# A fused retention and expert kernel: row scales written between two halves of the sums, expert loads moved up, and twenty products of the unit matrix ahead of the first expert

## The chip, the cores and the metric

The kernel runs on one core of one Trainium2 chip. The metric is the device time of one execution in microseconds (us). A core has five engines with an instruction queue of their own: TensorE (PE, with its weight loads as PEld), VectorE (DVE), ScalarE (ACT), GpSimd (POOL) and SyncE (SP), which issues most DMA transfers here. The 16 DMA engines are shared by all queues.

## The reference, cut to what matters

```python
# 1. retention: a decayed running state of k v^T, read with q     -> y [4, 8, 768, 64]
# 2. x = y as 3072 rows of 512; a first layer of 8 experts, each row goes to one:
logits = x @ w_gate;  e_idx = argmax(logits)
gate_w = softmax(logits)[e_idx];  eom = 1 / (1 + exp(-(x @ w_output_gate)))
for e in range(8):
    mask = e_idx == e
    out[mask] = gate_w[mask] * eom[mask, e] * (relu(x[mask] @ w1[e]) @ w2[e])
# 3. a second layer: slots from softmax(out @ phi) over the tokens, 8 experts over
#    the slots, and softmax(out @ phi) over the slots to put them together
```

All of it is float32. Layer 2 is never written out: the kernel folds `w2[e] @ phi` into one matrix per expert (`wp`), so that the logits of layer 3 come straight from the hidden units.

## The kernel before, in words

The order of all work is written out by hand: each engine runs its instructions in the order in which the Python code issues them, and waits on semaphores where data is missing.

**Stage A, up to about 115 us.** 24 tiles of 128 tokens go through the retention. For each group of three tiles the rows (`xr`) and 16 copies of the row's scale (`sv`, 64 bytes a row) are written to a DRAM table `xs` (`x_put`, `scale_put`). While the last tiles run, the first quarter of `w2[e] @ phi` is computed for all eight experts (`first_mm`, `first_copy`) into `fsum`, and written to a DRAM buffer `wps` in two halves of 512 KB.

**The handover, about 112 to 127 us.** `rank` and the products `lp` give each expert its list of tokens (`xidx`). GpSimd then gathers the rows of the first expert from `xs`, 128 rows at a time (`gather`, three tiles `xg`). After that stands a branch around a path for overfull experts, which is not taken (`tc.If(most > 0)`, L868): every engine reads a number and jumps over some hundreds of instructions. Behind the branch SP waits until the three gathers have landed (`after(..., gets[0])`, L1104) before it loads the other three quarters of the first expert's `w2` (`wq_load`, three loads `wt` of 512 KB). PE's first work behind the branch is `x_mm(0)`: twelve transposes `xps` of the scaled rows, four for each gathered tile. ACT and DVE split them into two parts (`x_split`, `xh` and `xl`).

**Stage B, the eight experts, about 127 to 370 us.** An expert has eight units of 128 hidden columns (unit g = 8e + f). A unit needs a weight load `r` (256 KB, `load_w(g + 3)`, three buffers), its split `wh`, `wl` on ACT and DVE (`split_w(g + 2)`, issued at the head of unit g), twelve matmuls `hps` on PE (`l1`, four quarters times three products, PSUM from a pool `ps_h` of two buffers), and a relu on ACT, which frees the PSUM buffer. ACT runs at the head of unit g: the split of unit g + 2, in units 4 and 5 two scalings of the next expert's rows (`x_scale`), and then the relu of unit g. For expert 0, `wq_mm(0)` multiplies the three loads `wt` behind unit 2 and frees their three buffers (`wup`). The loads of expert 1 into the same buffers are issued behind units 3 and 4, and `wq_mm(1)` stands behind unit 6. `part_load(1)` (`wpp`, 128 KB) reads the first quarter back from `wps`.

**Stage C, about 370 us to the end.** The second layer's experts on 32 slots, and the output.

Of the kernel before, what the change touches and what calls it, by code (L numbers as in the profile page):

```python
# [9 lines left out]
F32 = mybir.dt.float32  # L10
# [17 lines left out]
KD = DM // 128  # L28
# [10 lines left out]
IO, UMM, QA = 6, 2, 1  # L39
# [98 lines left out]
def retention_moe_kernel(ctx, tc, qt, kt, kn, vn, gates, moe_w1, moe_w2,  # L138
                         moe2_phi, moe2_w1, moe2_w2, consts, out, dbg=None):
    nc = tc.nc  # L140
# [11 lines left out]
    def con(name, shape=None):  # L152
        o, n = off[name]
        a = cs0[:, o:o + n] if o < ni else cs_a[0][:, o - ni:o - ni + n] if o < na else cs[:, o - na:o - na + n]
        if shape:
            a = a.rearrange("p (a b) -> p a b", b=shape)
        return a

    ident = con("ident")
# [36 lines left out]
    def load_er(k):  # L196
        if k < E:
            er.append(nc.values_load(ordi[0:1, k:k + 1], engines=[mybir.EngineType.SP], min_val=0, max_val=E - 1))
# [3 lines left out]
    def after(inst, earlier):  # L202
        for other in earlier:
            tc.add_manual_dep(inst.ins, other.ins.name,
                              mybir.DependencyInfo(mybir.DependencyClass.Sync, mybir.DependencyReason.DATA),
                              reason="order of transfers")
# [25 lines left out]
    def wq_load(k, q, n, pool, tag):  # L232
        t = pool.tile([128, n * FF], F32, tag=tag, name="wt")
        get = nc.sync.dma_start(out=t, in_=moe_w2[1, bass.ds(er[k], 1), :, q * FF:(q + n) * FF].rearrange("o p d -> (o p) d"))
        for h in range(n):
            wtt[k, q + h] = [t[:, h * FF + g * 256:h * FF + g * 256 + 256] for g in range(4)]
        return get
# [8 lines left out]
    def wq_add(k):  # L246
        nc.vector.tensor_tensor(out=parts[k], in0=wacc.pop(k), in1=parts[k], op=ALU.add)
# [69 lines left out]
    with ExitStack() as pa:  # L317
# [96 lines left out]
        def first_copy(e):  # L414
            nc.scalar.copy(out=fsum[:, e, :], in_=facc.pop(e))
# [133 lines left out]
        def bc(a, n, m=E):  # L549
            return a.unsqueeze(2).to_broadcast([128, n, m])  # L550
# [35 lines left out]
        def gate_scale(i):  # L586
            if i not in ENDS:
                return
            t, n = ENDS[i]
            sm = gs.pop(t)  # L590
            one_ = lambda k: sm[:, k, 0, 0:n]
            nc.vector.tensor_reduce(out=one_(8), in_=sm[:, 6, 0:n, :], axis=AX.X, op=ALU.add)
            nc.vector.tensor_scalar(out=one_(9), in0=one_(7), scalar1=1.0, scalar2=None, op0=ALU.add)
            nc.vector.scalar_tensor_tensor(out=one_(10), in0=one_(8), scalar=1e-9, in1=one_(9), op0=ALU.add, op1=ALU.mult)
            scl[t] = sc2.tile([128, 3, DX - DM], F32, tag="sv", name="sv")
            nc.vector.reciprocal(out=scl[t][:, 0:n, :], in_=bc(one_(10), n, DX - DM))
# [39 lines left out]
        def scale_put(i):  # L636

            if i not in ENDS:
                return
            t, n = ENDS[i]  # L640
            nc.sync.dma_start(out=xs[t * 128:(t + n) * 128, DM:DX].rearrange("(u p) o -> p u o", p=128), in_=scl.pop(t)[:, 0:n, :])
# [52 lines left out]
        i = NTILE - 1  # L694
# [5 lines left out]
        t, n = ENDS[i]  # L700
        past = [base[:, 0, 0:E], run[:, t, :]] + [oh[:, t + u, :] for u in range(n)]
        for o, w, terms in ((key, eights, past), (key, ones, [base[:, 1, 0:E]]), (counts, ones, past)):
            for m, b in enumerate(terms):
                nc.tensor.matmul(out=o, lhsT=w, rhs=b, start=(m == 0 and terms is past),
                                 stop=(m == len(terms) - 1 and (o is counts or terms is not past)), skip_group_check=True)
# [17 lines left out]
            first_mm(e)  # L723
        for e in range(4, E):
            first_copy(e)
        nc.sync.dma_start(out=wps[:, 4:E], in_=fsum[:, 4:E])
        gate_scale(i)
        scale_put(i)
        load_er(0)
        load_w(0)  # L730
        load_w(1)
# [16 lines left out]
        xg, gets = {}, {}  # L748
# [23 lines left out]
    with ExitStack() as pv:  # L772
# [95 lines left out]
        with tc.If(most > 0):  # L868
# [5 lines left out]
            for i in range(NTILE):  # L874
                places.append(nc.gpsimd.indirect_dma_start(
                    out=inv[:, :], out_offset=bass.IndirectOffsetOnAxis(ap=pos[:, i:i + 1], axis=0),
# [12 lines left out]
    wup = ctx.enter_context(tc.tile_pool(name="wup", bufs=KD - QA))  # L889
    with ExitStack() as pb:  # L890
        sp = pb.enter_context(tc.tile_pool(name="sp", bufs=1))
        ps_h = pb.enter_context(tc.tile_pool(name="ps_h", bufs=2, space=PSUM))
# [5 lines left out]
        def x_scale(e, j, vector=False):  # L898
            r = XT[e][j]
            x, s = xg[e][j][0:r, 0:DM], xg[e][j][0:r, DM:DM + 1]  # L900
            if vector:
                nc.vector.tensor_scalar(out=x, in0=x, scalar1=s, scalar2=None, op0=ALU.mult)
            else:
                nc.scalar.activation(out=x, in_=x, func=ACTF.Copy, scale=s)

        def x_mm(e, tags, blocks):

            ps = [ps_1.tile([128, C[e]], F32, tag=tag, name="xps") for tag in tags]
            for j, kk in blocks:
                r = XT[e][j]  # L910
                nc.tensor.transpose(out=ps[kk][:, j * 128:j * 128 + r],  # L911
                                    in_=xg[e][j][0:r, kk * 128:(kk + 1) * 128],
                                    identity=ident[0:r, 0:r])
            return ps
# [156 lines left out]
        def slot_acc(e):  # L1071
            nc.vector.scalar_tensor_tensor(out=acc, in0=acc, scalar=sms.pop(e)[:, 4:5], in1=slo.pop(e), op0=ALU.mult, op1=ALU.add)
# [28 lines left out]

        load_er(1)

        after(wq_load(0, QA, 1, wup, "wu"), gets[0])  # L1104
        for q in range(QA + 1, KD):
            wq_load(0, q, 1, wup, "wu")
        part_load(0)
        for j in range(len(XT[0])):
            if j == 1:
                split_w(0)  # L1110
            x_scale(0, j, j % 2 == 0)
        xps = x_mm(0, "ABCD", [(j, kk) for j in range(len(XT[0])) for kk in range(KD)])
        for ps in xps:
            x_split(0, ps)
        split_w(1)
        for g in range(G):
            e, f = divmod(g, KF)
            if f == 0:
                load_er(e + 2)
            if e + 1 < E and f < len(XT[e + 1]):  # L1120

                gather(e + 1, (f,))
                if f:
                    after(gets[e + 1][f], [relu[-1]])
            split_w(g + 2)
            if e and f == 1:

                if e > 1:
                    slot_acc(e - 2)
                logit_parts(e - 1)  # L1130
            if g < G - 3:
                load_w(g + 3)
            else:
                load_m2(wraw, "r1")
            if g > 3 and g % 2 and len(m2_t) < NPRE:
                load_m2(m2p, "m2", 2)
            if f in (4, 5) and e + 1 < E:
                for j in range(2 * f - 8, min(2 * f - 6, len(XT[e + 1]))):
                    x_scale(e + 1, j)
            if f == KF - 1 and e + 1 < E:  # L1140

                xps = x_mm(e + 1, "ABDr", sorted(((j, kk) for kk in range(KD) for j in range(len(XT[e + 1]))),
                                                 key=lambda b: XT[e + 1][b[0]] < 128))
                l1(g, lambda: [x_split(e + 1, ps) for ps in xps])
            else:
                l1(g)
            behind(e - 1, f)


            if g == UMM:  # L1150
                wq_mm(0, ps_1, "C")
                wq_add(0)
            if f == (1 if e else UMM):
                wq_turn(e, sp.tile([128, KF, NS], F32, tag="wp", name="wp"))
            if e + 1 < E:
                if f == (2 if e else 3):
                    part_load(e + 1)
                if e == 0 and f in (3, 4):
                    for q in ((1, 2), (3,))[f - 3]:
                        wq_load(1, q, 1, wup, "wu")  # L1160
                if f == (3 if e else 6):

                    wq_mm(e + 1, ps_1, "A" if e else "C")
                    wq_add(e + 1)
            if g == KF - 1:
                wq_load(2, 1, 1, wup, "wu")
                wq_load(2, 2, 1, wup, "wu")
            if g == KF:
                wq_load(2, 3, 1, wup, "wu")
            if e and e + 2 < E and 4 <= f < 7:  # L1170
                wq_load(e + 2, f - 3, 1, wup, "wu")
            elif G - 13 < g < G - 9:
                load_m2(wup, "wu", 2)
            if g == G - 6:
                load_w2(e, range(4), xp, "xy")
            if g >= G - 2:

                for i, tag in enumerate(("wh1", "wl1")):
                    load_w2(e, (2 * f - 8 + i,), whl, tag)
            if f == 4:  # L1180
                logits(e, 0)
            if f == 5:

                mask(e)
            if f >= 5:
                h_tr(e, 2 * f - 10)
                h_tr(e, 2 * f - 9)
        e = E - 1
# [30 lines left out]
        for kk in range(KD):  # L1219
            nc.tensor.matmul(out=ps4[:, kk, :], lhsT=acc[:, kk * 128:(kk + 1) * 128], rhs=sw,  # L1220
                             start=True, stop=True, skip_group_check=True)
# [171 lines left out]
```

## Time and profile before

| | |
|---|---|
| Time, median of 3 runs (lowest, highest) | 427.85 us (426.66, 427.98) |
| Time of the profiled execution | 427.91 us |
| Its span in the trace | 426.1 us, so 1.8 us lie around it |
| PE busy | 379.5 us (89% of the span) |
| DVE, ACT, POOL busy | 260.9, 165.6, 108.0 us |
| DMA | 132.96 MB, mean 312 GB/s |
| Granted TensorE clock, mean | 0.963 of full speed |
| Share of the chain that ended last | PE 73%, DVE 9%, DMA 7%, ACT 4% |

PE is the busiest engine and holds most of the chain that ended last. Two stretches stand out in its busy time by slices: one near 115 to 122 us, where it does nothing, and the tail beyond 355 us. The granted clock is at half (1.2 of 2.4 GHz) in the slices after the first of these. Times below are us from the start of the span.

### The profile page before, as it was taken

What the parts mean: (1) busy time and instruction counts of PE and PEld (TensorE: products, weight loads), DVE (VectorE), ACT (ScalarE), POOL (GpSimd) and SP (SyncE); (2) the same over time, 40 slices, a digit from 0 to 9 for tenths busy, and PEclk for the clock granted to TensorE, in tenths of its full rate; (3) what the DMA queues carried; (4) which work ended last, traced back from release to release, by engine and by line L of the source; (5) the groups of instructions that cost most, each with busy time, mean ns of one, the idle gap of its engine ahead of it and who ended that gap; (6) DMA issues with size and microseconds to landing.
All of it is one profiled execution on the core that took longest, in us unless ns stands there. A gap on an engine that the chain in (4) does not pass through costs nothing.

```text
span 426.1 us, 11539 instructions
## 1 busy us (share of the span) xinstructions
PE 379.5 (89%) x4407; PEld 284.7 (67%) x4407; DVE 260.9 (61%) x681; ACT 165.6 (39%) x368; POOL 108.0 (25%) x116
## 2 busy tenths in 40 slices
PE   2989999998639999999999999999999996799990
PEld 2877777786428777777877877787679872225560
DVE  1698989988723276575675664864757655414250
ACT  1532322223324365454545545543555421112232
POOL 2203333321033113043252431620612122020020
PEclk9999999999958999999999999999999999699996
DMA  7999999999958798977969969969778789999998
GB/s 270 403 420 334 307 314 338 304 280 327 251 161 316 222 368 287 385 279 237 403 225 329 376 203 357 358 192 386 248 223 338 238 263 318 388 398 407 392 346 289
DMA packets 68002, 132.96 MB, mean 312 GB/s; under 512 B 10628, under 2 KB 30082, under 8 KB 65634
## 3 DMA queue, kind: packets, MB, share of 16 engines
q1 hardware_dynamic: 61154, 120.17, 80.2%
q0 software_dynamic: 3344, 8.34, 6.5%
q10 hardware_dynamic: 3440, 3.63, 2.6%
q8 instruction: 36, 0.59, 0.6%
q14 instruction: 28, 0.23, 0.2%
HBM read 117.89 MB, written 14.25 MB: 310 GB/s over the span
## 4 chain that ended last, share of the span: by engine, by line
PE 73%; DVE 9%; DMA 7%; ACT 4%; issue 3%; SPq 1%; ACTq 1%; another core or an unknown queue 0%; POOL 0%; POOLq 0%; DVEq 0%
PE hps L933 30%; PE s L447 5%; PE o L480 5%; PE gps L1046 5%; PE fh L1246 4%; PE slo L1068 4%; PE so L1283 3%; PE lps L963 3%; PE wps L243 3%; PE o L471 2%; DMA r<-in_moe_w_dram 2%; DMA raw<-in_qt_dram 2%; PE xps L911 2%; PE st L494 2%; PE g L545 2%
## 5 line engine op out<-in xcount | busy, mean ns | idle before, releaser
L933 PE MATMUL hps<-xh,wh 128*128 128x416 f32 (+2 forms) x256 | 92.9, 363 | 0.1
L933 PE MATMUL hps<-xl,wh 128*128 128x416 f32 (+2 forms) x256 | 90.1, 352 | 0.3 <-DVE xl L921 0.2
L933 PE MATMUL hps<-xh,wl 128*128 128x416 f32 (+2 forms) x256 | 89.5, 350 | 0.0
L223 DVE TENSOR_TENSOR wl<-r,wh 128x512 fp32r<-128x512 f32 x64 | 43.4, 680 | 57.9 <-ACT wh L222 47.3
L938 ACT ACTIVATE h<-hps 128x416 f32<-128x416 f32 (+2 forms) x64 | 32.6, 510 | 68.7 <-PE hps L933 67.1
L222 ACT ACTIVATE wh<-r 128x512 fp32r<-128x512 f32 x64 | 40.2, 630 | 48.9 <-DMA r<-in_moe_w_dram 38.2
L933 PEld LDWEIGHTS hps<-xh,wh 128*128 128x128 f32 x256 | 48.7, 190 | 15.5 <-issue 13.4
L1029 POOL DMA_INDIRECT ctok<-ce,xidx x29 | 30.1, 1040 | 100.9 <-DVE ce L1026 94.5
L933 PEld LDWEIGHTS hps<-xl,wh 128*128 128x128 f32 x256 | 48.8, 190 | 2.2 <-DVE xl L921 1.2
L933 PEld LDWEIGHTS hps<-xh,wl 128*128 128x128 f32 x256 | 48.7, 190 | 0.6
L755 POOL DMA_INDIRECT xg<-xs,xidx x29 | 30.4, 1047 | 70.3 <-ACT h L938 49.5
L457 DVE TENSOR_TENSOR sS<-s,csa 128x512 f32<-128x512 f32 x48 | 30.4, 674 | 14.4 <-PE s L447 14.4
L447 PE MATMUL s<-raw 64*128 64x128 f32 x384 | 31.9, 301 | 8.0 <-DMA raw<-in_qt_dram 7.7
L945 DVE STREAM_TRANSPOSE hB<-h 128x416 f32<-128x416 f32 (+2 forms) x64 | 34.4, 576 | 0.0
L447 PEld LDWEIGHTS s<-raw 64*128 64x128 f32 x384 | 26.7, 201 | 10.7 <-DMA raw<-in_qt_dram 5.5
L480 PE MATMUL o<-sS,raw 128*64 128x128 f32 x384 | 27.1, 285 | 0.0
L512 ACT COPY xT<-o 128x512 f32<-128x512 f32 x24 | 13.9, 580 | 32.0 <-PE o L480 32.0
L429 POOL TENSOR_TENSOR k<-raw,cs 128x512 f32<-128x512 f32 x20 | 21.9, 1110 | 16.4 <-DMA raw<-in_qt_dram 11.1
L911 PE MATMUL xps<-cs,xg 128*128 128x128 f32 (+2 forms) x116 | 15.7, 285 | 9.2 <-ACT wh L222 7.9
L480 PEld LDWEIGHTS o<-sS,raw 128*64 128x64 f32 x384 | 21.2, 140 | 3.7 <-issue 3.4
L1046 PE MATMUL gps<-hB,pd 32*32 32x256 f32 x816 | 19.8, 394 | 3.6 <-DVE pd L1000 3.6
L911 PEld LDWEIGHTS xps<-cs,xg 128*128 128x128 f32 (+2 forms) x116 | 12.8, 148 | 13.6 <-issue 11.7
(178 smaller groups left out, 532.6 us busy)
## 6 DMA issues: line engine op xcount, KB each, us to landing
m<-in_moe_w_dram SPq DMA_DIRECT2D x41, 512.0 KB
wt<-in_moe_w_dram SPq DMA_DIRECT2D x32, 512.0 KB
r<-in_moe_w_dram SPq DMA_DIRECT2D x64, 256.0 KB
w<-in_moe_w_dram SPq DMA_DIRECT2D x64, 256.0 KB
m<-in_moe_w_dram SPq DMA_DIRECT2D x36, 256.0 KB
xs<-xr SPq DMA_DIRECT2D x32, 192.0 KB
raw<-in_kt_dram SPq DMA_DIRECT2D x5, 1024.0 KB
raw<-in_kn_dram SPq DMA_DIRECT2D x5, 1024.0 KB
```

The lines of the kernel that those rows point to most:

```text
L222: nc.scalar.activation(out=hi, in_=t, func=ACTF.Copy)
L223: nc.vector.tensor_tensor(out=lo, in0=t, in1=hi, op=ALU.subtract)
L447: nc.tensor.matmul(out=ps[h][:, p, :], lhsT=kq(i, p, 0)[r], rhs=kq(i, p, 1)[r], start=True, stop=True, tile_position=(64 * h, 0), skip_gro ...
L457: nc.vector.tensor_tensor(out=sS[i][:, h], in0=sps.pop((i, h)), in1=con("dm", 128)[:, 4 * h:4 * h + 4, :], op=ALU.mult)
L480: nc.tensor.matmul(out=o_at(i, p, h), lhsT=vals(i, 2 * p + h), rhs=s[:, h, p, :], start=(i % NCH == 0 and n < 4), stop=True, skip_group_ch ...
L755: gets.setdefault(e, []).append(nc.gpsimd.indirect_dma_start(out=t[0:r, :], out_offset=None, in_=xs[:, :], in_offset=bass.IndirectOffsetOn ...
L911: nc.tensor.transpose(out=ps[kk][:, j * 128:j * 128 + r], in_=xg[e][j][0:r, kk * 128:(kk + 1) * 128], identity=ident[0:r, 0:r])
L933: nc.tensor.matmul(out=ps, lhsT=a[:, kk * 128:(kk + 1) * 128], rhs=x[e][kk][:, 0:c], start=(n == 0), stop=(n == 11))
L938: relu.append(nc.scalar.activation(out=hs[g][:, 0:c], in_=ps, func=ACTF.Relu))
L945: nc.vector.transpose(out=hB[e][:, 0:NB[e], f, :], in_=hs[e * KF + f][:, 0:c].rearrange("p (b t) -> p b t", t=32))
L1029: put = nc.gpsimd.indirect_dma_start(out=ctok[:, :], out_offset=bass.IndirectOffsetOnAxis(ap=xidx[0:r, e, j:j + 1], axis=0), in_=cn[0:r, j ...
L1046: nc.tensor.matmul(out=ps[a][32 * j:32 * j + 32, :], lhsT=pd[q, b, :], rhs=hB[e][q, b].rearrange("p f t -> p (f t)"), start=(i == 0), stop ...
```

## The change

Four things are moved or added.

1. `gate_scale` and `scale_put` of the last group come ahead of the second half of `fsum` in SP's order.
2. The first load of expert 0's three `wt` waits for two gathers of the three.
3. Twenty float32 products of the 128x128 unit matrix with itself are put on PE between the branch and `x_mm(0)`. Nobody reads them. Their tile `idle` takes one of the two buffers of `ps_h`.
4. Expert 1's three loads `wt` are all issued right behind `wq_mm(0)`, in unit 2, not in units 3 and 4.

```diff
             first_copy(e)
+        gate_scale(i)
+
+        scale_put(i)
         nc.sync.dma_start(out=wps[:, 4:E], in_=fsum[:, 4:E])
-        gate_scale(i)
-        scale_put(i)
         load_er(0)
...
-        after(wq_load(0, QA, 1, wup, "wu"), gets[0])
+        after(wq_load(0, QA, 1, wup, "wu"), gets[0][:2])
...
             x_scale(0, j, j % 2 == 0)
+
+        idle = ps_h.tile([128, 512], F32, tag="h", name="idle")
+        for n in range(20):
+            nc.tensor.matmul(out=idle[:, n % 4 * 128:n % 4 * 128 + 128], lhsT=ident, rhs=ident, start=True, stop=True, skip_group_check=True)
         xps = x_mm(0, "ABCD", [(j, kk) for j in range(len(XT[0])) for kk in range(KD)])
...
             if g == UMM:
                 wq_mm(0, ps_1, "C")
                 wq_add(0)
+                for q in range(QA, KD):
+                    wq_load(1, q, 1, wup, "wu")
...
-                if e == 0 and f in (3, 4):
-                    for q in ((1, 2), (3,))[f - 3]:
-                        wq_load(1, q, 1, wup, "wu")
```

On PE, right behind the branch (L868, after the change L869), with `cs` the constants that hold the unit matrix, the changed kernel has:

```order
+L788 COMPARE_AND_BRANCH
+L788 UNCONDITIONAL_BRANCH
+L869 UNCONDITIONAL_BRANCH
+L1116 MATMUL idle<-cs_65 128x128 x20
+L912 MATMUL xps<-cs_65,xg 128x128 x12
+L934 MATMUL hps<-xh,wh_3555 128x384
```

The twenty products stand behind the branch and ahead of the twelve transposes; nothing else moves on PE here.

On SP, at the end of stage A, with `xs<-sv` the scales and `wps<-fsum` the two halves of the sums:

```order
 L649 DMA xs<-xr 32x12x128 x4
 L721 DMA wps<-fsum 128x1024
-L726 DMA wps<-fsum 128x1024
 L641 DMA xs<-sv 128x3x16
+L729 DMA wps<-fsum 128x1024
 L198 TENSOR_LOAD ordi
```

The scales go past one transfer of 512 KB. On DVE no row moves.

On SP, in units 2 to 5 of expert 0 (`r` the weight loads, `wt` the loads for `wq_mm(1)`, `wpp` the first quarter), before, with the load of unit 6 as `r_3706` and that of unit 7 as `r_3733`:

```order
L214 DMA r_3665<-in_moe_w_dram 128x512 [waits DMAHW3_49,DVE_49]
L214 DMA r_3706<-in_moe_w_dram 128x512 [waits DMAHW4_49,DMAHW1_49,DVE_49]
L949 DMA wpp<-wps 128x256 [waits DMAHW5_49,DVE_49]
L234 DMA wt<-in_moe_w_dram 128x1024 [waits DMAHW6_49,PE_49]
L234 DMA wt<-in_moe_w_dram 128x1024 [waits DMAHW7_49,PE_49]
L214 DMA r_3733<-in_moe_w_dram 128x512 [waits DMAHW2_49,DMAHW0_49,Activation_49]
L234 DMA wt<-in_moe_w_dram 128x1024 [waits PE_49]
L214 DMA r_3763<-in_moe_w_dram 128x512 [waits DMAHW3_49,DVE_49]
```

and after the change, with the load of unit 6 as `r_3733` and that of unit 7 as `r_3756`:

```order
L214 DMA r_3686<-in_moe_w_dram 128x512 [waits DMAHW3_49,DVE_49]
L234 DMA wt<-in_moe_w_dram 128x1024 [waits DMAHW5_49,DMAHW4_49,PE_49]
L234 DMA wt<-in_moe_w_dram 128x1024 [waits DMAHW6_49,PE_49]
L234 DMA wt<-in_moe_w_dram 128x1024 [waits DMAHW7_49,PE_49]
L214 DMA r_3733<-in_moe_w_dram 128x512 [waits DMAHW1_49,DVE_49]
L950 DMA wpp<-wps 128x256 [waits DMAHW0_49,DVE_49]
L214 DMA r_3756<-in_moe_w_dram 128x512 [waits DMAHW2_49,Activation_49]
L214 DMA r_3784<-in_moe_w_dram 128x512 [waits DMAHW3_49,DVE_49]
```

The load of unit 6 was ahead of all three `wt` and is now behind them; the load of unit 7 was ahead of one and is now behind all three.

## Rows read from the trace of the kernel before

**Rows 1.** Time by windows: busy us of five engines, clock, DMA share, GB/s.
```profile
115.00:120.00 5.00, 0.00 (x0) 0.00 (x0) 2.04 (x10) 0.00 (x0) 2.02 (x2) 0.83 0.69 197
131.00:132.00 1.00, 1.00 (x5) 1.00 (x5) 0.00 (x0) 0.12 (x1) 0.00 (x0) 0.50 1.01 385
132.00:133.00 1.00, 1.00 (x7) 1.00 (x6) 0.00 (x0) 0.37 (x1) 0.36 (x1) 1.00 1.01 383
128.50:134.50 6.00, 6.00 (x27) 6.00 (x26) 2.00 (x4) 1.51 (x4) 1.01 (x1) 0.71 1.02 386
```

**Rows 2.** The branch's line, PE alone: duration in ns (min/median/max), first to last start.
```profile
L868 PEldq EVENT_SEMAPHORE  x2: 51/51/51, 121.5 to 121.7; - x2
L868 PEldq COMPARE_BRANCH  x1: 4183/4183/4183, 117.2 to 117.2; - x1
```

**Rows 3.** Timeline of the handover: start us, us, engine, line, what, [idle before <-releaser].
```profile
112.94 0.36 SPq L726 DMA_DIRECT2D wps<-fsum  x1
113.39 0.39 SPq L641 DMA_DIRECT2D xs<-sv  x1
115.25 0.19 DVE L746 TENSOR_REDUCE xidx<-lx 128x4 int32<-128x32 f32 x1
117.68 1.27 POOL L755 DMA_INDIRECT xg<-xs,xidx  x1 [11.56 <-DMA r<-in_moe_w_dram]
125.64 0.48 DVE L902 TENSOR_SCALAR xg<-xg 128x512 f32<-128x512 f32 x1 [2.02 <-DMA xg<-xs,xidx]
125.83 1.42 SPq L234 DMA_DIRECT2D wt<-in_moe_w_dram  x3
126.19 1.11 PE L911 MATMUL xps<-cs,xg 128*128 128x128 f32 x4 [1.23 <-DVE xg L902]
127.37 0.69 PE L933 MATMUL hps<-xh,wh 128*128 128x384 f32 x1
```

**Rows 4.** DMA packets between 115.0 and 115.5 us.
```profile
DMA packets 364, 0.10 MB, mean 205 GB/s; under 512 B 344, under 2 KB 344, under 8 KB 364
```

**Rows 5.** Timeline of PE, units 0 and 1 of expert 0, and the next transposes.
```profile
131.32 0.52 PE L933 MATMUL hps<-xh,wl 128*128 128x384 f32 x1
131.64 0.51 PE L933 MATMUL hps<-xh,wh 128*128 128x384 f32 x1
...
150.25 1.92 PE L911 MATMUL xps<-cs,xg 128*128 128x128 f32 x16
```

**Rows 6.** The page's costliest groups: the scores of stage A.
```profile
L447 PE MATMUL s<-raw 64*128 64x128 f32 x384 | 31.9, 301 | 8.0 <-DMA raw<-in_qt_dram 7.7
```

**Rows 7.** The chain that ended last, where stage C begins: start us, us, what.
```profile
370.82 8.77 PE fh L1246 x64
```

**Rows 8.** Time by windows, a little later in stage C.
```profile
374.00:376.00 2.00, 2.00 (x24) 0.63 (x20) 0.00 (x0) 0.00 (x0) 1.70 (x2) 0.91 1.02 405
```

**Rows 9.** Timeline of PE, units 2 to 8.
```profile
136.10 1.50 PE L243 MATMUL wps<-wt,phi 128*32 128x256 f32 x24
...
144.92 0.33 PE L933 MATMUL hps<-xh,wh 128*128 128x384 f32 x1
...
147.09 1.07 PE L243 MATMUL wps<-wt,phi 128*32 128x256 f32 x16
149.68 0.64 PE L243 MATMUL wps<-wt,phi 128*32 128x256 f32 x8 [1.52 <-DMA wt<-in_moe_w_dram]
...
161.24 0.45 PE L984 MATMUL lsum<-ll,same_r 128*128 128x384 f32 x1 [0.37 <-DVE ll L971]
```

**Rows 10.** Timeline of ACT and SP, units 1 to 4.
```profile
134.47 0.63 ACT L222 ACTIVATE wh<-r 128x512 fp32r<-128x512 f32 x1 [2.09 <-DMA r<-in_moe_w_dram]
...
140.33 0.63 ACT L222 ACTIVATE wh<-r 128x512 fp32r<-128x512 f32 x1
...
142.08 0.48 ACT L938 ACTIVATE h<-hps 128x384 f32<-128x384 f32 x1
...
144.32 0.33 SPq L234 DMA_DIRECT2D wt<-in_moe_w_dram  x1
```

More of the change, by code (lines that the diff above doesn't have):

```diff
@@ L725, in retention_moe_kernel @@
             first_copy(e)
-        nc.sync.dma_start(out=wps[:, 4:E], in_=fsum[:, 4:E])
         gate_scale(i)
         scale_put(i)
+        nc.sync.dma_start(out=wps[:, 4:E], in_=fsum[:, 4:E])
         load_er(0)
```

## The prediction

> **What bounds the kernel now.** I read first the chain that ended last: 73% of it is PE. Then PE's waits between 122 us and the end: behind the handover they sum to little before stage C, and the only one that is a wait for a transfer is 1.52 us in expert 0 [rows 9]. So a microsecond that PE gains or loses between 122 and 150 us reaches the end, unless a wait behind it takes it up. Third, the windows of the handover [rows 1]. PE does nothing from 115 us on. The clock stands at 0.83 on the mean of 115 to 120 us, so it fell from 2.4 to 1.2 GHz with (1 - 0.83) / 0.5 x 5 = 1.7 us left, at 118.3 us; it is still at half in 131 to 132 us and at full in 132 to 133 us. Fourth, why PE is idle. The page puts PE's wait down to missing rows, but the branch's own line shows more: PE's compare-and-branch began at 117.2 us and took 4.18 us, and its last instruction there begins at 121.7 us [rows 2]. Until then PE can run nothing that stands behind the branch. Last I read the timeline from there to 150 us for the two chains that the moved transfers touch.
>
> **The change, part by part.**
>
> *Scales first.* The first gather starts at 117.68 us [rows 3]. Its list is ready at 115.25 + 0.19 = 115.44 us, so it waits for something else. The row names a weight load, which the gather doesn't read; it does read `xs`, and the scales are the last to be written there. They were issued at 113.39 us, and their 384 packets of 64 bytes move only at 115.0 to 115.5 us (344 small packets) [rows 4], behind the 512 KB issued at 112.94 us. In front of that half they leave at about 112.95 us and save its transfer, 512 KB at 386 GB/s [rows 1] = 1.4 us. They can't save more than 117.68 - 115.44 = 2.2 us, nor less than the 0.45 us of the earlier issue; I take 1.2 us. All three gathers come that much sooner, the third at 124.4 for 125.64 us [rows 3]. Alone this would move `hps` up by as much; here PE isn't free by then (below), so it counts as nothing. Behind the scales the second half of the sums is 0.4 us later, and nobody reads it before unit 3.
>
> *Two gathers for three.* SP issues expert 0's `wt` loads at 125.83 us, behind the third gather [rows 3]. With two it can do so as soon as it is past the branch, about 122.6 us: 3.2 us sooner, and with them the `r` loads queued behind. The wait for `r` at 134.47 us [rows 10] was ACT's, and PE ran through it, so the gain is nothing. The price could be that 1.5 MB share the engines with the third gather. A delay of it up to 2 us stays hidden behind the idle products, which last longer; without them it would count.
>
> *Twenty products.* A float32 product that isn't a transpose shows as two records: the scores are 8 calls in each of 24 tiles, and 384 records [rows 6]. So there are 40 records of 128 columns. Their nearest row is the float32 transpose with the same 128x128 weights: 16 in 1.92 us at full clock with 0.27 us for the last, 0.11 us apart [rows 5]; four in 1.11 us at half clock, (1.11 - 0.42) / 3 = 0.23 us apart [rows 3]. I take 0.22 and 0.11 us. PE can begin them at about 121.9 us [rows 2], not at 115 us, and the clock is at half by then. When does it rise? In this stage it rose at 132.0 us after work without long gaps from 126.19 us, 5.8 us; in stage C `fh` begins at 370.82 us [rows 7], and the mean of 0.91 between 374 and 376 us [rows 8] puts the rise at 374.36 us, 3.5 us. These are my bounds; I take the middle, 4.6 us, so 126.5 us. By then 4.6 / 0.22 = 21 records are done, the other 19 take 2.1 us: the end is 128.6 us (128.0 and 129.2 by the bounds). If all 40 ran at half clock it would be 130.7 us, at full clock 126.3 us.
>
> Then come the twelve transposes, whose rows have all landed: eight at 0.11 us, and from the ninth to the first `hps` 127.37 - 126.19 = 1.18 us at half clock [rows 3], say 1.0 at full. So `hps` starts at 128.6 + 0.9 + 1.0 = 130.5 us, 3.1 us later than before, but at full clock. Unit 0 before ran from 127.37 to 131.64 us at 0.32 us a matmul [rows 5]; unit 1, nearly all at full clock, took 0.32 + 11 x 0.175 = 2.2 us and ended at 133.9 us. After: 24 x 0.175 = 4.2 us, end 134.7 us. **Loss 0.8 us (0.3 to 1.4).** The products give the clock back, and take more time at the head of PE's queue than the clock returns.
>
> *Expert 1's loads at unit 2.* They wait for the buffers that `wq_mm(0)` frees from 136.10 us on [rows 9], so they are issued from about 136.7 us, for 144.32 us of the third one before [rows 10]. That removes the wait of 1.52 us at 149.68 us. But the load of unit 6 is now behind them on SP's queue. What is behind it in turn: ACT splits unit 6 ahead of scaling two tiles and of unit 4's relu, and unit 6's matmuls need the PSUM buffer which that relu frees. From the split's start to the relu's end it is 142.56 - 140.33 = 2.2 us [rows 10]. When does that load land? The nearest row is the same sequence in expert 0: three `wt`, `wpp` and an `r`, first issue at 125.83 us, and ACT gets its `r` at 134.47 us: 8.6 us. At 386 GB/s [rows 1] the 1.8 MB and 0.4 MB of gathers beside them take 5.8 us, with 0.8 us to the first packet 6.6 us. I take 7.6: it lands at 144.3 us (143.3 to 145.3), the relu ends at 146.6, and unit 6 can start at 146.7 us where PE is ready at 144.92 us [rows 9]: a new wait of 1.8 us (0.8 to 2.8). From unit 6's start to the next transposes it is 147.09 - 144.92 for the unit and 1.5 for `wq_mm(1)` without a wait [rows 9], 3.7 us, so they start at 150.4 us for 150.25 us. **The wait moves: 0.15 us (-0.85 to +1.15).** All these times shift by the loss above alike.
>
> *Behind it.* The 1.5 MB have left the crowded stretch behind 145 us, so the `lsum` wait of 0.37 us at 161.24 us [rows 9], whose split waited for a late load, should go: **-0.4 us (0 to -0.4).** Stage C shifts with PE.
>
> **Sum.** 427.91 (this execution, 0.06 us above the median) + 0.8 + 0.15 - 0.4 = **428.5 us**: no change that can be told. About 0.3% of this kernel, 1.3 us, is what a measurement can tell; within it means 426.6 to 429.1 us. By the terms' bounds the time lies between 427.0 and 430.5 us.
>
> **A rule to weigh.** The branch row says 4.18 us on PE [rows 2]. The Trainium skill, "Advanced Engine Details and Errata", section Control Flow Timing, gives a compare-and-branch about 108 ns. By that the products would start at 117.4 us, be done by 122 us at full clock, and the sum would be that of the first rival below. This case's trace disagrees: 4183 ns for this one, which jumps far.
>
> **Rivals.**
> 1. *The products fill the wait.* The jump is short after the change, and PE runs all 40 records at 0.11 us from 117.4 to 121.8 us, before the clock falls and the rows come. Then the earlier gathers count too: `hps` at 124.4 + 0.5 + 1.1 = 126.0 us, at full clock, and unit 1 ends at 130.2 us for 133.9: -3.7, with the other terms 424.0 us. For it: the edit's place in the code. Against it: 4.18 us in the row, and nothing in the change shortens the jump. The Trainium skill's figure above is the rule for it. Chance 0.03.
> 2. *The products are cheaper.* If each were one record, 20 at 0.22 us end at 126.3 us, `hps` starts at 128.2, unit 1 ends at 132.4 us: -1.5, total 426.2 us. The counts of records speak against it. With other small gains (unit 6's load in time, a rise at 3.5 us), chance of this side 0.11.
> 3. *Slower: unit 6's load.* It lands 8.6 us or more behind the first issue; then each further 1 us is 1 us of PE. With +1.15 and the upper bound of the products, 430.1 us. It decides where the load lands past 145.5 us. For it: the row that measured 8.6 us. Against it: the engines moved 386 GB/s in the later part of that stretch, and at that rate 6.6 us are enough. Chance 0.16.
> 4. *Slower: the clock stays down.* All 40 records at half clock, end 130.7 us, `hps` at 132.6, unit 1 at 136.8 us or later: +2.9, total 430.6 us. It decides where the rise comes later than 7 us. Both rises in the trace came sooner. Chance 0.12.
>
> **Numbers.** Likeliest: within 0.3%, chance 0.58, 428.5 us, its own range 427.0 to 429.1. Faster 0.14 (rivals 1 and 2), slower 0.28 (3 and 4). The range that holds 8 in 10 is 426.4 to 430.3 us: it leaves out the first rival and half of the fourth.
>
> **What will show it.** The first gather starts near 116.5 us. The products begin near 121.9 us, 40 records, half clock, and the rise comes near 126.5 us. `hps` starts between 129.9 and 131.1 us. `wt` of expert 1 leaves near 137.5 us, no wait at `wq_mm(1)`, and in its place PE waits ahead of unit 6 for the relu of unit 4. The prediction is wrong if the products begin before 120 us, if a product costs one record, or if PE enters unit 6 without a wait.

## The result

The changed kernel took **429.88 us** (median of 9 executions, 428.94 to 430.70) beside 427.85 us for the kernel before (9 executions, 424.94 to 428.61): ratio **1.006, 95% interval 1.0035 to 1.0084**. It is slower by 0.6%. The forecast was 428.5 us and no difference that can be told. A few executions of a kernel are over 1.5% slower than its fastest and are left out of the ratios; the trace of the run with scales and gathers is of such an execution, so its places are listed below and nothing rests on them.

The handover went nearly as worked out. Timeline of the changed kernel, POOL, SP and PE (start us, us, engine, line, what, number, idle time ahead), where [rows 3] show the kernel before:

```profile
112.80 0.38 SPq L641 DMA_DIRECT2D xs<-sv  x1
113.28 0.44 SPq L729 DMA_DIRECT2D wps<-fsum  x1
114.54 0.32 PE L739 MATMUL lp<-lcol,lrow 128*128 128x32 bf16 x6 [1.02 <-DVE lrow L634]
116.43 1.27 POOL L756 DMA_INDIRECT xg<-xs,xidx  x1 [10.45 <-DVE lim L767]
121.96 6.11 PE L1116 MATMUL idle<-cs 128*128 128x128 f32 x40 [7.11 <-PEq L869]
122.34 2.39 SPq L234 DMA_DIRECT2D wt<-in_moe_w_dram  x3
129.76 0.44 PE L934 MATMUL hps<-xh,wh 128*128 128x384 f32 x1 [0.38 <-ACT xh L921]
136.62 1.50 PE L243 MATMUL wps<-wt,phi 128*32 128x256 f32 x24
```

The scales stand ahead of the second half of the sums, the first gather starts at 116.43 for 117.68 us, SP issues expert 0's `wt` loads at 122.34 for 125.83 us. The `lp` row is PE's last work in stage A. The products begin at 121.96 us, 40 records, behind a branch that holds PE as before. The branch's line (PE alone, ns):

```profile
L869 PEldq COMPARE_BRANCH  x1: 4317/4317/4317, 117.2 to 117.2; - x1
```

`wq_mm(0)` starts at 136.62 for 136.10 us [rows 9]: 0.5 us lost up to there. The rest is lost in the next 17 us. PE's waits between 120 and 156 us (us in total, times, longest):

```profile
PE idle L1116 <- PEq L869: 7.1, 1, 7.1
PE hps L934 <- ACT h L939: 3.0, 1, 3.0
```

The wait of 1.52 us at `wq_mm(1)` is gone, and one of 3.0 us stands ahead of unit 6. The chain that ended last shows why (start us, us, what):

```profile
136.69 1.48 PE wps L243 x24
...
138.19 0.44 DVE wpp L247
...
139.02 0.49 DVE wl L223
139.51 6.70 DMA r<-in_moe_w_dram
...
146.30 0.63 ACT wh L222
146.93 0.42 ACT xg L905
...
147.44 0.55 ACT xg L905
...
148.06 0.47 ACT h L939
...
148.58 3.91 PE hps L934 x12
```

Unit 6's load `r` leaves at 139.51 us, behind expert 1's three `wt` loads, and takes 6.70 us. It leaves late because SP runs its queue in order: SP stood for 3.8 us at the first `wt`, until `wq_mm(0)` freed its buffer (SP's waits, us in total, times, longest):

```profile
SPq L234 <- PE wps L243: 4.1, 2, 3.8
```

The buffer of unit 6's own load was free earlier, when DVE had split unit 3 (133.61 + 0.69 = 134.30 us). ACT splits unit 6's load at 146.30 us, scales two tiles, and only then runs unit 4's relu (`h`), which frees the PSUM buffer that unit 6 needs. PE's timeline from there:

```profile
148.58 0.52 PE L934 MATMUL hps<-xh,wh 128*128 128x384 f32 x1 [2.97 <-ACT h L939]
152.41 1.50 PE L243 MATMUL wps<-wt,phi 128*32 128x256 f32 x24
153.85 1.92 PE L912 MATMUL xps<-cs,xg 128*128 128x128 f32 x16
```

Two things are to be seen. Unit 6's twelve matmuls take 152.41 - 148.58 = 3.83 us, where before they took 147.09 - 144.92 = 2.17 us [rows 9]; and the next transposes start at 153.85 us, 3.60 us later than the 150.25 us of [rows 5]. Windows of the same kernel tell why the twelve are slow (busy us of five engines, clock, DMA share, GB/s):

```profile
120.00:125.00 5.00, 3.04 (x14) 3.07 (x15) 1.40 (x3) 1.35 (x2) 0.36 (x1) 0.51 0.70 192
145.00:150.00 5.00, 2.03 (x9) 1.71 (x8) 1.62 (x3) 3.70 (x7) 0.00 (x0) 0.88 0.79 286
150.00:155.00 5.00, 5.00 (x44) 3.94 (x43) 2.42 (x6) 2.17 (x5) 0.00 (x0) 0.78 0.60 185
360.00:365.00 5.00, 2.38 (x102) 1.48 (x104) 2.65 (x9) 1.54 (x5) 0.00 (x0) 1.00 1.00 345
365.00:370.00 5.00, 2.94 (x30) 1.05 (x22) 2.32 (x8) 0.00 (x0) 0.00 (x0) 1.00 1.05 395
```

Behind the wait the clock falls to half: (1 - 0.88) x 2 x 5 = 1.2 us of it up to 150 us, and 2.2 us more up to 152.2 us. Behind 150 us the shift stays: +2.65 us at expert 2's transposes, +2.90 us at 355 us. At 370.8 us it is gone (370.81 us for 370.82 us [rows 7]), because in this one execution the clock stayed at full between 360 and 370 us (last two rows), where in the execution before it was at 0.57 and 0.75:

```profile
360.00:365.00 5.00, 3.70 (x92) 1.40 (x78) 1.21 (x3) 0.65 (x2) 0.00 (x0) 0.57 1.05 390
365.00:370.00 5.00, 3.50 (x22) 1.01 (x14) 1.86 (x7) 0.00 (x0) 0.00 (x0) 0.75 1.05 386
```

Rows of the two traces, the first of the kernel before, the others of the changed kernel:

```profile
179.12 1.89 PE L911 MATMUL xps<-cs,xg 128*128 128x128 f32 x16
181.77 1.89 PE L912 MATMUL xps<-cs,xg 128*128 128x128 f32 x16
370.81 8.67 PE L1250 MATMUL fh<-m,siT 128*32 128x512 f32 x64 [0.35 <-ACT siT L1226]
392.57 0.23 DVE L1303 CAST c<-two 128x128 fp32r<-128x128 f32 x1 [2.87 <-DMA two<-ctok]
393.35 1.13 PE L1312 MATMUL ctps<-ident_r,c 128*96 128x128 f32 x12 [0.51 <-DVE c L1303]
```

The span is still longer, 427.6 for 426.1 us, but by another cause: near 393 us PE waits for `c`, whose input from DRAM (`ctok`) came late. The second trace of the changed kernel has no such wait, and its span is 430.6 us. So the span of one execution does not show what the change costs.

In the runs below the clock in that stretch changes from one execution to the next, of the same kernel too. So places up to 180 us are read from the traces, and times from the medians.

### The profile page after: what moved, and what is told of

It reads as the page before. It is cut to its first block, busy times and chain, and to the rows that moved or that the text cites. A ratio compares the mean times of both kernels' runs of the same rounds, so it can differ in the third digit from the quotient of the medians.

```text
span 427.6 us, 11620 instructions
## 1 busy us (share of the span) xinstructions
PE 380.2 (89%) x4447; PEld 289.0 (68%) x4447; DVE 260.4 (61%) x681; ACT 164.6 (39%) x368; POOL 107.3 (25%) x116
## 4 chain that ended last, share of the span: by engine, by line
PE 44%; DMA 18%; DVE 3%; ACT 3%; issue 1%; ACTq 1%; SPq 0%
PE hps L934 24%; DMA r<-in_moe_w_dram 10%; DMA w<-in_moe_w_dram 4%; PE slo L1069 3%; PE so L1287 3%; PE fh L1250 2%; PE lps L964 2%; PE gps L1047 2%; PE wps L243 2%; DMA two<-ctok 2%; PE xps L912 1%; PE idle L1116 1%; DMA m<-in_moe_w_dram 1%; DVE wl L223 1%; ACT wh L222 1%
## 5 line engine op out<-in xcount | busy, mean ns | idle before, releaser
L922 DVE TENSOR_TENSOR xl<-xps,xh 128x416 fp32r<-128x416 f32 (+2 forms) x32 | 16.7, 575 | 5.9 <-ACT xh L921 5.7
L977 POOL TENSOR_SCALAR msk<-cs,rt 128x416 f32<-128x416 f32 (+2 forms) x8 | 13.7, 1715 | 23.4 <-DVE srun L1003 23.3
```

## The experiments

All were timed beside the kernel before on the same chip, in three groups; its medians there were 427.05, 429.45 and 426.85 us. The table gives the ratio with its interval, the start of `wq_mm(0)` (136.10 us before), PE's wait ahead of unit 6, its wait at `wq_mm(1)`, and the start of expert 1's transposes (150.25 us before).

| kernel | ratio (95%) | wq_mm(0) | unit 6 | wq_mm(1) | transposes |
|---|---|---|---|---|---|
| before | 1 | 136.10 | 0 | 1.5 | 150.25 |
| the whole change | 1.006 (1.0035 to 1.0084) | 136.62 | 3.0 | 0 | 153.85 |
| the same again | 1.0097 (1.0067 to 1.0127) | 137.70 | 3.5 | 0 | 155.43 |
| loads not moved | 1.0004 (0.9968 to 1.0039) | 138.26 | 0 | 0 | 150.68 |
| moved loads alone | 1.0062 (1.0025 to 1.0099) | 134.58 | 3.6 | 0 | 153.69 |
| scales and gathers | 0.9957 (0.9921 to 0.9992) | 136.68 | 0 | 0 | 149.30 |
| twenty products alone | 1.0004 (0.9967 to 1.0041) | 136.89 | 0 | 0.2 | 149.74 |
| unit 6's load first | 1.0007 (0.9978 to 1.0036) | 137.35 | 0 | 0 | 149.78 |
| that, no products | 0.9941 (0.9902 to 0.9979) | 135.53 | 0 | 0 | 147.96 |
| that, eight products | 0.9943 (0.9910 to 0.9977) | 134.82 | 0 | 0 | 147.25 |
| eight, loads not moved | 0.9951 (0.9917 to 0.9986) | 134.34 | 0 | 0.2 | 147.22 |
| whole, wait filled | 1.0049 (1.0019 to 1.0079) | 137.22 | 0.3 | 0 | 153.17 |
| scales alone | 0.9985 (0.9948 to 1.0021) | 134.15 | 0 | 1.5 | 148.52 |
| two gathers alone | 0.9971 (0.9938 to 1.0003) | 136.71 | 0 | 0 | 149.28 |

**The change without its moved loads.** Expert 1's `wt` loads stand in units 3 and 4 again; the other three edits stay.

```diff
                 wq_add(0)
-                for q in range(QA, KD):
-                    wq_load(1, q, 1, wup, "wu")
...
+                if e == 0 and f in (3, 4):
+                    for q in ((1, 2), (3,))[f - 3]:
+                        wq_load(1, q, 1, wup, "wu")
```

> The changed kernel with expert 1's three loads put back to units 3 and 4. Theory L (the moved loads cost: unit 6's weight load is late, PE waits 3.0 us for unit 4's relu and then runs unit 6 at half clock): no wait ahead of unit 6, the 1.5 us wait at wq_mm(1) is back, and the time is 0.5 us above before, from the products alone. Theory P (the products cost the 2 us that were measured): still 2 us above before.

Ratio 1.0004, and PE enters unit 6 without a wait. What the change loses is gone with the moved loads. The wait of 1.5 us at `wq_mm(1)`, expected back, did not come: the third `wt` was there in time. From `wq_mm(0)` to the transposes it is 12.42 us here, and 17.23 us with the moved loads.

**The moved loads alone.** The kernel before with only those lines moved.

> Before with one part of the change, the three loads of expert 1 in unit 2. Theory L: PE waits 2.5 to 3 us ahead of unit 6, the clock may fall there, and the time is 2 us above before. Theory P: no difference to before.

Ratio 1.0062, as large as that of the whole change. The timeline of ACT and PE in it:

```profile
144.91 0.63 ACT L222 ACTIVATE wh<-r 128x512 fp32r<-128x512 f32 x1 [5.99 <-DMA r<-in_moe_w_dram]
147.19 0.69 PE L933 MATMUL hps<-xh,wh 128*128 128x384 f32 x1 [3.62 <-ACT h L938]
...
151.33 2.42 PE L243 MATMUL wps<-wt,phi 128*32 128x256 f32 x24
```

Again `r` is late, PE waits, and then runs at half clock: unit 6 takes 151.33 - 147.19 = 4.14 us, and a `wq_mm` that takes 1.50 us at full clock [rows 9] takes 2.42 us.

**Scales and gathers.** The first two edits without the other two.

```diff
+        gate_scale(i)
+        scale_put(i)
         nc.sync.dma_start(out=wps[:, 4:E], in_=fsum[:, 4:E])
-        gate_scale(i)
-        scale_put(i)
...
-        after(wq_load(0, QA, 1, wup, "wu"), gets[0])
+        after(wq_load(0, QA, 1, wup, "wu"), gets[0][:2])
```

> Before with the scales ahead of the second half and two gathers for three, without products and with expert 1's loads in units 3 and 4. Both theories: the gathers start 1.2 us sooner and hps starts 1.2 us sooner, near 126.2 us, at half clock; 1 to 2 us below before. If the third gather is slowed by the loads that now run beside it, hps starts as late as before and nothing is gained.

Ratio 0.9957: faster by 0.4%. These two edits do bring something where no products stand ahead of the rows.

**The twenty products alone.** The kernel before with only the three lines of `idle`.

> Before with the twenty products alone. Theory L: the products run from 122 to 128 us, hps starts near 130.4 us at full clock, unit 1 ends 0.5 us later than before, and the time is 0.5 us above before. Theory P: 2 us above before.

Ratio 1.0004. `wq_mm(0)` starts 0.79 us later, the wait behind it shrinks from 1.52 to 0.2 us, and the transposes start 0.5 us sooner: the loss is taken up by a wait that this kernel, with three gathers, had in its trace before.

**Unit 6's load first.** The whole change, with the load that was made late put ahead of the three loads that made it late.

```diff
-            if g < G - 3:
+            if g == UMM + 1:
+                pass
+            elif g < G - 3:
                 load_w(g + 3)
...
                 wq_add(0)
+                load_w(UMM + 4)
                 for q in range(QA, KD):
                     wq_load(1, q, 1, wup, "wu")
```

> The whole change, with unit 6's load handed to the queue of SP ahead of the three loads of expert 1's rows in unit 2 instead of behind them in unit 3. Theory L (the moved loads cost the time, by making unit 6's load late): unit 6's load lands before its use, the 3.0 us wait of TensorE ahead of unit 6 and the half clock behind it go, and the time is 2 to 3 us below the whole change, near or a little below the kernel before (ratio 0.996 to 1.001). Theory P (the twenty products and what they push back cost it): nothing changes, ratio 1.006 as for the whole change.

Ratio 1.0007. SP's and PE's timeline:

```profile
135.06 0.33 SPq L214 DMA_DIRECT2D r<-in_moe_w_dram  x1
138.05 2.70 SPq L234 DMA_DIRECT2D wt<-in_moe_w_dram  x3
148.34 1.50 PE L243 MATMUL wps<-wt,phi 128*32 128x256 f32 x24
149.78 1.92 PE L912 MATMUL xps<-cs,xg 128*128 128x128 f32 x16
```

The load leaves at 135.06 us, 2.3 us ahead of `wq_mm(0)`; in the changed kernel it left 2.9 us behind it. No wait ahead of unit 6, none at `wq_mm(1)`, and the transposes start 12.4 us behind `wq_mm(0)` instead of 17.2. The order on SP's queue was the cost, not the loads themselves. The time agrees, though the intervals of this run and of the whole change just touch (1.0036 and 1.0035). How much of the delay was the late issue, and how much the 1.5 MB ahead of it in the transfers, was not separated.

**Unit 6's load first, no products.**

> As the run with unit 6's load first, and without the twenty products: scales between the halves, two gathers instead of three, and the moved loads behind unit 6's load. Theory L: close to the scales and gathers alone (ratio 0.994 to 0.999). Theory that the moved loads also cost by what they take from the transfers of units 3 to 5: ratio over 1.000, with waits ahead of those units.

Ratio 0.9941: 0.66% below the same kernel with twenty products (426.66 for 429.60 us, medians on one chip; the intervals of the two ratios meet at 0.9979 and 0.9978). So the products cost more than the 0.5 us that the trace of the whole change shows. The run also shows a limit to what a gain ahead of 150 us is worth. ACT and PE, a little later:

```profile
158.73 0.63 ACT L222 ACTIVATE wh<-r 128x512 fp32r<-128x512 f32 x1 [3.13 <-DMA r<-in_moe_w_dram]
159.26 0.47 ACT L971 ACTIVATE ls<-lps 128x384 fp32r<-128x384 f32 x1
159.79 0.44 PE L985 MATMUL lsum<-ls,same_r 128*128 128x384 f32 x1 [1.31 <-ACT ls L971]
```

The transposes start 2.29 us sooner than before, `lsum` only 160.43 - 159.79 = 0.64 us: PE comes sooner, but ACT holds `ls` behind the split of a weight load that has not landed, while the DMA engines are busy all the time (share 0.92 and 1.01 in 150 to 160 us). The loss of the changed kernel met no such wait: 2.65 of its 3.60 us were left at expert 2's transposes.

**Eight products.** The whole change with unit 6's load first and `range(8)` instead of `range(20)`; and the same with expert 1's loads left in units 3 and 4.

> The whole change with unit 6's load first and eight products instead of twenty. The records of the products, 40 for 20, then end near 125.4 us instead of 128.6, before the first rows are there, so the transposes are not pushed back, and the clock may still rise with them. If the products' push of 0.5 to 0.8 us is a loss that reaches the end, this is 0.5 to 0.8 us below the run with unit 6's load first; if the wait behind it takes it up, the two are the same within 0.3%.

> The first two edits and eight products, with expert 1's loads where they were before the change. If the moved loads bring nothing even behind unit 6's load, this is like the run with eight products and unit 6's load first (ratio 0.9943) within 0.3%. If the moved loads bring something there (the wait for their last one, ahead of unit 7, stands again once the units before it end sooner), this is 0.3 to 0.5% longer than it.

Ratios 0.9943 and 0.9951. PE in the first of the two:

```profile
121.78 3.78 PE L1116 MATMUL idle<-cs 128*128 128x128 f32 x16 [6.65 <-ACTq L869]
125.36 2.20 PE L912 MATMUL xps<-cs,xg 128*128 128x128 f32 x12
127.94 0.44 PE L934 MATMUL hps<-xh,wh 128*128 128x384 f32 x1 [0.38 <-issue]
134.82 1.50 PE L243 MATMUL wps<-wt,phi 128*32 128x256 f32 x24
```

The rows come when the products end, and the clock is up for unit 0 all the same. With eight products the time is 2.9 us below that with twenty (426.67 for 429.60 us), where 0.5 to 0.8 us were expected. `wq_mm(0)` starts at 134.3 to 134.8 us, 2.5 to 3.0 us sooner than the 137.35 us with twenty. Of that, no gain over the kernel without products is left in the time (0.9943 and 0.9951 for 0.9941). And whether expert 1's loads are moved makes no difference that can be told once unit 6's load stands ahead of them (with twenty products too: 1.0007 and 1.0004).

The products do bring the clock back sooner. Its mean in 125 to 130 us is 0.76 to 1.00 in the eight traces with products, with eight as with twenty, and 0.50 to 0.60 in the five without.

**The wait filled.** The whole change, with thirteen more products on PE between units 5 and 6; they add work that nothing reads.

```diff
+            if g == 5:
+                fill = ps_1.tile([128, 512], F32, tag="B", name="fill")
+                for n in range(13):
+                    nc.tensor.matmul(out=fill[:, n % 4 * 128:n % 4 * 128 + 128], lhsT=ident, rhs=ident, start=True, stop=True, skip_group_check=True)
```

> The whole change with thirteen more products of the unit matrix on TensorE between unit 5 and unit 6, where it waits 3.0 us for unit 6's load; they add work that nothing reads. Theory W (the wait takes TensorE's clock down, and the half clock behind it costs 1.8 us more): the granted clock stays at full speed behind the wait, unit 6's twelve products take about 2.1 us instead of 3.9, and the time is about 1.8 us below the whole change (ratio about 1.002). Rival (the fall of the clock has to do with something else at that place, or the products themselves take up what they save): unit 6 still runs at half clock, or the time stays at ratio 1.006.

Timeline and windows:

```profile
146.04 3.06 PE L1187 MATMUL fill<-cs 128*128 128x128 f32 x26
149.42 0.45 PE L934 MATMUL hps<-xh,wh 128*128 128x384 f32 x1 [0.32 <-ACT h L939]
151.74 1.50 PE L243 MATMUL wps<-wt,phi 128*32 128x256 f32 x24
145.00:150.00 5.00, 4.68 (x36) 4.49 (x36) 0.77 (x2) 2.86 (x6) 0.00 (x0) 1.00 0.88 324
150.00:155.00 5.00, 5.00 (x51) 3.78 (x49) 3.96 (x8) 2.91 (x6) 0.00 (x0) 1.00 0.76 246
```

The clock stays at full, and unit 6 takes 151.74 - 149.42 = 2.32 us. So it was the idle stretch that took the clock down. The nine other traces without the wait agree: their mean clock between 134 and 355 us is 1.00. From `wq_mm(0)` to the transposes it is 15.95 us, for 17.23 and 17.73 us in the two traces of the whole change: 1.3 to 1.8 us less. In the time this can't be told: ratio 1.0049, where 1.002 was expected, and its interval overlaps that of the whole change.

**Scales alone; two gathers alone.** The two parts of the run with scales and gathers.

> The scales between the sums' halves alone; the other three edits undone. The first gather starts about 1.2 us sooner, and expert 0's rows and the transposes behind them with it. Theory S (the gain of the first two edits together, ratio 0.9957, comes from the earlier rows, since without the twenty products TensorE is free to begin sooner): ratio 0.994 to 0.999. Rival (it comes from the loads that start behind two gathers instead of three): no difference, ratio 0.997 to 1.003.

> The two gathers instead of three alone; the other edits undone. Expert 0's four loads of the wt rows start about 3.2 us sooner. Theory S: no measurable difference (ratio 0.997 to 1.003), since the loads were there in time before. Rival: the gain of the first two edits is here, ratio 0.994 to 0.998.

Ratios 0.9985 and 0.9971, and neither interval excludes 1. Their product, 0.9956, fits the 0.9957 of both together, but which of the two brings how much stays open.

**The whole change again.**

> The whole change again, beside the others on this chip: ratio 1.003 to 1.009 to the kernel before, and the wait of about 3 us ahead of unit 6 with half clock behind it again.

Ratio 1.0097, a little above what was expected. Two of its waits and two windows:

```profile
PE hps L934 <- ACT h L939: 3.5, 1, 3.5
PE gps L1047 <- DVE pd L1001: 3.1, 1, 3.1
150.00:152.00 2.00, 1.80 (x7) 1.81 (x8) 1.31 (x3) 2.00 (x5) 0.00 (x0) 0.69 0.50 133
360.00:365.00 5.00, 3.05 (x96) 1.67 (x96) 1.99 (x8) 0.89 (x3) 0.00 (x0) 0.74 1.00 364
```

The same wait ahead of unit 6, and the half clock behind it. The wait at `gps`, in stage C, is taken up in the last section.

## Why the prediction was wrong

The step that failed is *Expert 1's loads at unit 2*, "The wait moves: 0.15 us (-0.85 to +1.15)". From `wq_mm(0)` to the next transposes it was 14.15 us before [rows 5, 9] and 17.23 us after: **+3.1 us** in place of +0.15 (+3.6 in the second trace of the change, and +5.0 in that of the moved loads alone). Beside the run that differs in the moved loads alone (12.42 us) it is **+4.8 us**; in the time 0.6%, 2.4 us, is left of that, and where the rest went was not followed. The new wait was foreseen, with the path that leads to it. One size was off, one term was missing, and one gain was counted that another edit brings.

- The load was taken to land 7.6 us behind the first moment at which `wt` could be issued, at 144.3 us. It landed at 146.2 us, 8.9 us behind the first `wt` (issued at 137.32 us). It left at 139.51 us, 2.2 us behind that one, and took 6.70 us from there. Its relu ended at 148.5 for 146.6 us, so the wait was 3.0 us for 1.8. The nearest row, 8.6 us, was the better guess than the mean with a transfer time at 386 GB/s. That is past the 145.5 us at which the third rival decides. Its 430.1 us is close to the 429.88 us measured in part by luck: it had this landing, but neither the clock behind the wait nor the wait that the second edit removes.
- The wait was priced as idle time alone. It also took the clock down, and unit 6 lost 3.83 - 2.17 = 1.7 us more behind it. No term of the sum had this; the filled wait shows it in the trace.
- The wait of 1.52 us at `wq_mm(1)` was counted as a gain of the move. In the runs that kept the loads in place it was 1.5 us with the scales alone and 0.2 us with the twenty products alone, both with three gathers as before; with two gathers it was 0, 0 and 0.2 us (two gathers alone, loads not moved, eight products). So in the changed kernel the second edit, counted at nothing, goes with its end, and the move had nothing left to gain there (0.9943 with the loads moved, 0.9951 without). Why two gathers end it was not tested.

With 1.2 for the wait and 1.7 for the clock, 0.15 becomes 3.1 us; with the 1.52 us that were not the move's to gain it becomes 4.6 of the 4.8 us.

The measured 429.88 us lies inside the range of 426.4 to 430.3 us, near its end. What failed is its centre, a change that can't be told.

*Twenty products*, "Loss 0.8 (0.3 to 1.4)": near in its places (begin 121.96 for 121.9 us, 40 records, the clock's rise at 124.9 us and 126.9 us in the two traces for 126.5, `hps` at 129.76 and 130.83 us for 130.5), and in the run without the moved loads the time is that of before. But the loss is larger than the term. The rise at 132 us on which it was sized is that of one execution; with the scales alone the mean clock of 125 to 130 us is 0.60, so there it rose near 129 us. Counted from PE's last `lp` row in stage A, which itself starts between 113.57 and 115.31 us (114.54 after, 114.67 before), `wq_mm(0)` starts 22.1 to 23.3 us later in the six traces with twenty products, 19.5 to 21.6 in the five without, and 19.8 and 20.0 with eight. Behind the same other edits, the twenty cost 0.9941 to 1.0007 and 0.9957 to 1.0004, 0.5 to 0.7% or 2 to 3 us (the intervals of the first pair just meet, those of the second overlap); alone they cost nothing that can be told. *Scales first* and *Two gathers for three* are worth 0.4% together without the products. For the scales the reason for counting nothing was that PE is held by the products, and the runs fit it: the products spend what the two edits gain. For the two gathers it was that PE runs through the wait for `r`; the wait at `wq_mm(1)` was not thought of.

*Behind it*, "-0.4 us": the stretch from the transposes to expert 2's gave back 3.60 - 2.65 = 0.95 us; the `lsum` wait is gone as said.

Two smaller readings are off. Three `wt`, `wpp` and an `r` are 1.97 MB, not 1.8, so with the gathers they take 6.1 us at 386 GB/s, not 5.8. And the profile puts PE's first wait down to `ACT wh`, not to missing rows.

The branch: PE's record of it is 4317 ns in the changed kernel and 3.7 to 5.2 us in all 14 traces, so the first rival is out. The Trainium skill, "Advanced Engine Details and Errata", section Control Flow Timing, has about 108 ns for a compare-and-branch; PE's record does not agree.

Put on one after the other, the edits bring -0.4% (scales, gathers), +0.5% (twenty products) and +0.6% (loads that make unit 6's load late), against the 0.6% measured and 1.0% measured again. These steps add up by the way they are taken. Each alone, the ratios are 0.9957, 1.0004 and 1.0062; their product is 1.002, so the parts do not simply add, though the intervals are too wide to be sure.

## What to carry to other kernels

When loads are moved up on a queue, price the load that they now stand ahead of, and through every instruction that waits behind it on its engine: here one `r` load, behind loads that waited for a buffer, held up a relu that has nothing to do with it. A new wait on TensorE in dense work costs its idle time and can cost a stretch of half clock behind it: here 1.7 us on top of 3.0. Before a wait is counted as a gain, ask whether another part of the change already ends it. And do not take the moment of a clock rise from a single execution: it lay between 124.9 and 133 us here. What PE loses at the head of a stretch may vanish in the next wait, and what it gains may run into a late load.

## What was not expected of the hardware

A wait of 3.0 to 3.6 us of TensorE in an otherwise busy stretch was followed by half clock three times out of three: for 3.4 us in both traces of the changed kernel, and for 6.8 us (146.4 to 153.2) with the moved loads alone. With products in the place of the wait it did not fall. But a wait of that length does not always take the clock down: in stage C PE waits at `gps` in every trace. In the eight traces that count where that wait is 3.1 us, the clock fell within about 1 us of its end in five and stayed at full in three; in the five where it is 3.6 or 3.7 us, it fell each time. The changed kernel is on both sides: after 360 us its mean clock is 1.00 in the first trace and 0.74 in the second. So the clock of a stretch is not the kernel's own: between 360 and 370 us one execution ran at 0.57 and 0.75, another at full. It may be part of why one kernel's executions lie up to 7 us apart here (425.03 to 431.91 us for the kernel before, 35 executions): their times and their mean clocks go together in part (correlation -0.56).
